# Numerator and transposes side by side in a linear-attention loop, with wo in the numerator's banks

## The chip, the cores and the metric

One Trainium2 chip, one of its cores. The metric is the device time of one execution in microseconds; what is compared is the median over several runs. The engines are named as the profile names them: PE is TensorE, DVE is VectorE, ACT is ScalarE, POOL is GpSimd, SP is SyncE, which issues most of the transfers.

## The reference

Two blocks on a sequence of 2048 tokens with 512 channels. The change touches the first one alone.

```
h = x + A(layernorm(x));   h2 = h + B(layernorm(h))

A: q, k, v = x @ wqkv, 32 heads of 16
   phi(p) = [softmax(p @ w_phi), softmax(-(p @ w_phi))]      per head, 32 features
   num = phi_q (phi_k^T v);   den = phi_q . sum_s(phi_k) + 1e-6
   A = (num / den) @ wo
B: u = gelu(layernorm(h)^T @ w1 + b1)   over tokens, F = 1792;   y = (u @ w2 + b2)^T
```

## The kernel before

The tokens are cut into 16 tiles of 128 (NT = 16). The weights wk and wq are folded with w_phi beforehand. Nearly every product is made as three matmuls of rounded halves (mm3: high x high, high x low, low x high), 128x512 each, so that a projection of one tile is 4 x 3 = 12 matmuls. In the profile these stand at L62, L63 and L64 whatever the product, and are told apart by the tile they write.

**First part (to about 142 us).** For each tile the projections of k (pk_ps), of v (pv) and of some q (pu), the features of k and the products kvp of k and v (L207). Six tiles of q are made here and four more at its end. Of a tile's q logits VectorE takes the maximum and minimum of each head's 16 features (mx, mn), subtracts the maximum (eq), GpSimd makes the negative side (negate, L159 and L160), ScalarE the exponentials (q_exp, L171), and VectorE their sums (q_sum, L216, two reduces), into one PSUM bank that holds eight tiles' sums in turn.

**The loop (142 to about 262 us)** has 19 turns, "it" from 0, in an order written by hand: each engine does its instructions in the order of the code. In one turn these steps stand in the code for different tiles:

- s_tr(it): 16 transposes of the features on TensorE, by halves of 64 rows, into the PSUM tile tn (L528), and two copies of them to pht on ScalarE (L530).
- s_num(it-1): the numerator, 16 small matmuls of 64x32 (32 passes in the profile), also into the PSUM tile tn (L546); ScalarE makes the high half oh (L550), VectorE the low half ol (s_ol, L555).
- s_wo(it-2): 12 matmuls with wo into po (a PSUM bank of its own), and s_h(it-2): VectorE adds the residual and the row's sum (L571), and SP stores it.
- s_moments, s_rstd and s_hn of tile it-3: the second layernorm, on ScalarE, GpSimd and ScalarE again (L577 to L587), and the halves hs of the result (L57 and L58).
- s_den(it+2): the denominator's inverse w, six operations on VectorE in a row (L451 to L457) after GpSimd's ez (s_ez, L442); s_pq multiplies it into the features on GpSimd (L460).
- one more projection of q while there are any (six tiles), and from it = 4 on fill: matmuls of block B's first product, 6 for each tile and pair of columns (pu<-hs). Their weights come by stream: a load on SP, the high half whi on ScalarE (L607) and the low half wlo on VectorE (flush, L599).

VectorE's operations are mixed by turns(): one of the list of ol, logits and sums, one of the denominator, and so on. The PSUM pool ps_t has one buffer of two banks for tn, so transposes and numerator take turns in it and the copies out lie between them.

**After the loop** come the rest of block B's first product and its second product (py), whose code is not changed.

Of the kernel before, what the change touches and what calls it, by code (L numbers as in the profile page):

```python
# [26 lines left out]
SUMS = 8  # L27
# [6 lines left out]
def block_kernel(ctx: ExitStack, tc: tile.TileContext, x, xT, wT, phic, wo, w1, b1, w2, b2,  # L34
# [34 lines left out]
    ps_s = aq.enter_context(tc.tile_pool(name="ps_s", bufs=1, space=PSUM, side="right"))  # L69
    sums = ps_s.tile([P, SUMS, NPR, 2, 2], F32, name="smq")  # L70
# [4 lines left out]
    kvS = wqp.tile([P, 4, 64], F32, name="kvS")  # L75
    wqp.tile([P, 504], F32, name="pad")
# [15 lines left out]
    ps_kv = a1.enter_context(tc.tile_pool(name="ps_kv", bufs=1, space=PSUM))  # L92
    kvp = ps_kv.tile([P, 4, 64], F32, name="kvp")
# [117 lines left out]
    def q_sum(t):  # L211

        assert t < SUMS or t - SUMS in W, "a tile's sums would go where others are still wanted"
        SQ[t] = sums[:, t % SUMS]
        e = signs(EQ[t])
        return [lambda c=c: nc.vector.reduce_sum(SQ[t][:, :, 1 - c], e[:, :, c], axis=AX.X) for c in range(2)]  # L216
# [227 lines left out]
    def s_den(t):  # L444


        tz = az.tile([P, NPR, 2, 2], F32, name="tz")
        den = az.tile([P, NPR, 2], F32, name="den")
        W[t] = az.tile([P, NPR, 2, 2], F32, name="w", bufs=3)
        other = SQ[t]  # L450
        return [lambda: nc.vector.reduce_sum(tz.rearrange("p g c h -> p (g c h)"), heads(EZ[t]), axis=AX.X),  # L451
                lambda: nc.vector.scalar_tensor_tensor(tz[:, :, 0], other[:, :, 1], 1e-6, tz[:, :, 0],
                                                       op0=ALU.mult, op1=ALU.add),
                lambda: nc.vector.tensor_mul(tz, other, tz),
                lambda: nc.vector.reduce_sum(den, tz.rearrange("p g c h -> p g h c"), axis=AX.X),
                lambda: nc.vector.reciprocal(den, den),
                lambda: nc.vector.tensor_mul(W[t], other, den.unsqueeze(2).to_broadcast([P, NPR, 2, 2]))]  # L457
# [3 lines left out]

    def lead(it, mm):

        if 0 <= it + 3 < NT:
            s_ez(it + 3)
        negate()
        for _ in range(mm):
            q_mm()
        q_exp(0)
# [24 lines left out]
    run(s_den(0))  # L494
# [7 lines left out]
    run(s_den(1))  # L502
# [15 lines left out]
    ps_o = a2.enter_context(tc.tile_pool(name="ps_o", bufs=1, space=PSUM, reuse_waits="tile"))  # L518
    HN, HT, PHT, OS, PO, VE = {}, {}, {}, {}, {}, {}

    def s_tr(t):

        PHT[t] = ak.tile([P, NG, P], F32, name="pht")
        ptr = ps_t.tile([P, 2, 4, P], F32, name="tn").rearrange("p r c (a s) -> p r (c a) s", a=2)
        for g in range(NG):
            for r in range(2):
                half = slice(r * 64, r * 64 + 64)
                nc.tensor.transpose(ptr[:, r, g, :], EQ[t][half, g, :], ident[half, half])  # L528
# [3 lines left out]
    def s_kv():  # L532

        pt = ps_o.tile([P, 2, P], F32, name="po")
# [4 lines left out]
    def s_num(t):  # L539

        pn = ps_t.tile([P, 2, 4, P], F32, name="tn")[:, :, 0:2]
        for b in range(2):
            for c in range(4):
                for r in range(2):
                    rows, cols = slice(64 * r, 64 * r + 64), slice(32 * c, 32 * c + 32)
# [11 lines left out]
    def s_wo(t):  # L557
        oh, ol, _ = OS.pop(t)
        PO[t] = po = ps_o.tile([P, D], F32, name="po")
# [34 lines left out]
    LATER = []  # L594

    def flush():
        while LATER:
            wl_, raw, wh_ = LATER.pop(0)
            LO.append(nc.vector.tensor_sub(wl_, raw, wh_).ins)  # L599

    def stream(src, k0, n, c0, w):
# [5 lines left out]
        nc.scalar.activation(wh_, raw, AF.Copy)  # L607
        LATER.append((wl_, raw, wh_))
# [23 lines left out]

    for it in range(NT + 3):
        if 0 <= it < NT:
            s_x(it)
        if 0 <= it - 1 < NT:
            s_num(it - 1)
        if 0 <= it - 3 < NT:
            s_moments(it - 3)
        if 0 <= it - 2 < NT:  # L640
            s_wo(it - 2)
        if it == 1:
            run(q_logits(0))
            q_mm()
        if 0 <= it < NT:
# [3 lines left out]
        if 0 <= it + 1 < NT:  # L649
# [223 lines left out]
```

## Time and profile before

| what | value |
|---|---|
| median of 3 runs | 530.51 us (530.28 to 531.23) |
| the profiled execution | 530.51 us, its span 528.70 us |
| TensorE busy | 521.9 us, 99% of the span, 4000 matmul passes |
| VectorE, ScalarE, GpSimd busy | 72%, 52%, 44% |
| granted TensorE clock | 0.999 |
| median from issue to landing | wraw 2.9 us, h 3.6 us, out<-h 2.0 us |

A row of a timeline gives the start in us from the span's start, the duration, the engine, the line, the operation, what it writes and reads, and in brackets how long the engine had been idle and what ended that. Matmuls are pipelined: their durations overlap, and the distance between starts is what counts. A busy share is an average over parts with different limits.

### The profile page before, as it was taken

What the parts mean: (1) busy time and instruction counts of PE and PEld (TensorE: products, weight loads), DVE (VectorE), ACT (ScalarE), POOL (GpSimd) and SP (SyncE); (2) the same over time, 40 slices, a digit from 0 to 9 for tenths busy, and PEclk for the clock granted to TensorE, in tenths of its full rate; (3) what the DMA queues carried; (4) which work ended last, traced back from release to release, by engine and by line L of the source; (5) the groups of instructions that cost most, each with busy time, mean ns of one, the idle gap of its engine ahead of it and who ended that gap; (6) DMA issues with size and microseconds to landing.
All of it is one profiled execution on the core that took longest, in us unless ns stands there. A gap on an engine that the chain in (4) does not pass through costs nothing.

```text
span 528.7 us, 10143 instructions
## 1 busy us (share of the span) xinstructions
PE 521.9 (99%) x4000; PEld 445.5 (84%) x4000; DVE 379.6 (72%) x680; ACT 272.7 (52%) x460; POOL 231.3 (44%) x190
## 2 busy tenths in 40 slices
PE   8999999999999999999999999999999999999996
PEld 7888888887877777777788888888899999999996
DVE  6993999876899888863426424825668878887784
ACT  6998834525247777676657323526444243343340
POOL 2589699876999988994335000000001101101110
PEclk9999999999999999999999999999999999999999
DMA  8644310012303223333255333533014555535631
GB/s 308 192 129 119 87 35 21 1 49 93 102 1 100 72 97 114 121 121 120 81 183 156 104 98 98 165 115 81 20 41 113 141 146 145 131 125 121 160 75 47
DMA packets 45488, 55.86 MB, mean 106 GB/s; under 512 B 3968, under 2 KB 33024, under 8 KB 45440
## 3 DMA queue, kind: packets, MB, share of 16 engines
q1 hardware_dynamic: 43136, 51.38, 31.0%
q0 software_dynamic: 2016, 3.67, 5.1%
q8 instruction: 31, 0.51, 0.4%
q10 hardware_dynamic: 288, 0.17, 0.1%
q14 instruction: 17, 0.14, 0.1%
HBM read 46.81 MB, written 8.39 MB: 104 GB/s over the span
## 4 chain that ended last, share of the span: by engine, by line
PE 96%; DVE 2%; ACT 0%; issue 0%; DVEq 0%
PE py L767 26%; PE pu L62 13%; PE pu L63 12%; PE pu L64 12%; PE po L62 3%; PE pv L63 3%; PE pv L64 3%; PE pv L62 3%; PE po L63 3%; PE po L64 3%; PE pk_ps L62 2%; PE pk_ps L64 2%; PE pk_ps L63 2%; PE tn L546 2%; PE tn L528 2%; PE kvp L207 2%
## 5 line engine op out<-in xcount | busy, mean ns | idle before, releaser
L805 POOL DMA_DIRECT2D out<-ot x14 | 12.5, 998 | 211.7 <-DVE ot L803 211.7
L767 PE MATMUL py<-uf,whi 128*128 128x256 f32 x560 | 96.2, 283 | 0.0
L62 PE MATMUL pu<-hs,whi 128*128 128x512 f32 x224 | 88.0, 396 | 0.0
L57 ACT ACTIVATE whi<-wraw 128x1792 fp32r<-128x1792 f32 x28 | 47.7, 1704 | 77.9 <-PE py L767 67.2
L63 PE MATMUL pu<-hs,whi 128*128 128x512 f32 x224 | 87.5, 391 | 0.0
L64 PE MATMUL pu<-hs,wlo 128*128 128x512 f32 x224 | 87.0, 390 | 0.2 <-DVE wlo L599 0.2
L767 PEld LDWEIGHTS py<-uf,whi 128*128 128x128 f32 x560 | 83.3, 192 | 0.0
L599 DVE TENSOR_TENSOR wlo<-wraw,whi 128x512 fp32r<-128x512 f32 x56 | 45.5, 823 | 48.7 <-ACT whi L607 48.3
L767 PE MATMUL py<-uf,wlo 128*128 128x256 f32 x280 | 69.9, 283 | 0.0
L58 DVE TENSOR_TENSOR wlo<-wraw,whi 128x1792 fp32r<-128x1792 f32 x28 | 56.6, 2022 | 17.2 <-ACT whi L57 17.1
L607 ACT ACTIVATE whi<-wraw 128x512 fp32r<-128x512 f32 x56 | 34.4, 626 | 45.5 <-PE pu L63 41.4
L64 PEld LDWEIGHTS pu<-hs,wlo 128*128 128x128 f32 x224 | 42.1, 188 | 9.6 <-DVE wlo L599 0.6
L62 PEld LDWEIGHTS pu<-hs,whi 128*128 128x128 f32 x224 | 42.0, 188 | 9.4
L767 PEld LDWEIGHTS py<-uf,wlo 128*128 128x128 f32 x280 | 49.7, 192 | 0.0
L63 PEld LDWEIGHTS pu<-hs,whi 128*128 128x128 f32 x224 | 42.1, 188 | 8.3
L442 POOL TENSOR_TENSOR ez<-eq,zB 128x1024 f32<-128x1024 f32 x16 | 39.3, 2458 | 3.9 <-ACT zB L489 3.9
L767 PE MATMUL py<-un,whi 128*128 128x256 f32 x224 | 38.4, 283 | 0.0
L195 POOL TENSOR_TENSOR pk<-pk,sk 128x1024 f32<-128x1024 f32 x16 | 31.0, 1942 | 9.8 <-DVE sk L194 9.0
L767 PEld LDWEIGHTS py<-un,whi 128*128 128x128 f32 x224 | 33.2, 192 | 0.1
L530 ACT ACTIVATE pht<-tn 128x512 f32<-128x512 f32 x32 | 17.4, 596 | 29.5 <-PE tn L528 29.5
L460 POOL TENSOR_TENSOR eq<-eq,w 128x1024 f32<-128x1024 f32 x16 | 31.0, 1940 | 3.0 <-DVE w L457 3.0
L199 POOL TENSOR_TENSOR zacc<-zacc,pk 128x1024 f32<-128x1024 f32 x13 | 31.3, 2407 | 0.6
(165 smaller groups left out, 1176.0 us busy)
## 6 DMA issues: line engine op xcount, KB each, us to landing
wraw<-in_w SPq DMA_DIRECT2D x112, 256.0 KB, 2.9
xraw<-in_xT SPq DMA_DIRECT2D x16, 256.0 KB, 3.0
xh<-in_x SPq DMA_DIRECT2D x16, 256.0 KB, 2.7
h<-in_x SPq DMA_DIRECT2D x16, 256.0 KB, 3.6
out<-h SPq DMA_DIRECT2D x16, 256.0 KB, 2.0
out<-ot POOLq DMA_DIRECT2D x14, 256.0 KB, 4.8
wraw<-in_wT SPq DMA_DIRECT2D x12, 256.0 KB, 5.0
wo<-in_wo SPq DMA_DIRECT2D x4, 256.0 KB, 3.6
```

What stands on the lines that cost most here:

```text
L57: nc.scalar.activation(hi, src, AF.Copy)
L58: lo_engine.tensor_sub(lo, src, hi)
L62: nc.tensor.matmul(o, ah, bh, start=first, stop=False)
L63: nc.tensor.matmul(o, ah, bl, start=False, stop=False)
L64: nc.tensor.matmul(o, al, bh, start=False, stop=last)
L195: nc.gpsimd.tensor_mul(heads(PK[t]), heads(PK[t]), sk.unsqueeze(2).to_broadcast([P, 2 * H, DH]))
L199: nc.gpsimd.tensor_add(zacc, zacc, PK[t])
L442: nc.gpsimd.tensor_mul(EZ[t], EQ[t], zB)
L460: nc.gpsimd.tensor_mul(heads(EQ[t]), heads(EQ[t]), W[t].rearrange("p g c h -> p (g c h)").unsqueeze(2).to_broadcast([P, 2 * H, DH]))
L599: LO.append(nc.vector.tensor_sub(wl_, raw, wh_).ins)
L607: nc.scalar.activation(wh_, raw, AF.Copy)
L767: nc.tensor.matmul(o, a[x], b[:, y], start=start and i == 0, stop=stop and i == 2, skip_group_check=True)
```

## The change

- The PSUM pools of the loop are now ps_t, two banks for the transposes (tr), and ps_n, two banks for the numerator (pn); s_wo writes po into the numerator's banks. The bank of the sums is given up: the sums of all 16 tiles go to SBUF.
- In a turn s_num(it-1) and s_tr(it) stand directly behind each other; then six matmuls of other work (half a q projection, or a fill), then s_wo(it-1), the tile of the numerator just made, then the other six or twelve, then s_h(it-1). The moments and what follows are those of it-2. Q_TURNS spreads six q projections over eight turns, in halves of six matmuls.
- s_den keeps its temporary values in PSUM, in the transposes' banks once they are copied out (before the loop in a bank of the pool ps_d), and its six operations now follow each other, between the two reduces of the sums.
- A streamed weight's high half is made in his(), on ScalarE after s_hn, and its low half in flush at the turn's end, after s_h.

The lines' numbers move with it: the denominator stands at L454 to L462, s_pq at L465, whi at L600 and wlo at L606.

```diff
...
 V_NOT = (0, 1, 11)
-SUMS = 8
+Q_TURNS = ((0, 1), (0, 1), (0, 1), (0, 1), (0,), (1,), (0,), (1,))
 LAG = 4
...
     ps_q = ctx.enter_context(tc.tile_pool(name="ps_q", bufs=2, space=PSUM, side="right"))
-    ps_s = aq.enter_context(tc.tile_pool(name="ps_s", bufs=1, space=PSUM, side="right"))
-    sums = ps_s.tile([P, SUMS, NPR, 2, 2], F32, name="smq")
     wqp = aq.enter_context(tc.tile_pool(name="wqp", bufs=1, side="right"))
...
     kvS = wqp.tile([P, 4, 64], F32, name="kvS")
+    sums = wqp.tile([P, NT, NPR, 2, 2], F32, name="smq")
     wqp.tile([P, 504], F32, name="pad")
...
     ps_kv = a1.enter_context(tc.tile_pool(name="ps_kv", bufs=1, space=PSUM))
+    ps_d = a1.enter_context(tc.tile_pool(name="ps_d", bufs=1, space=PSUM))
     kvp = ps_kv.tile([P, 4, 64], F32, name="kvp")
...
-        assert t < SUMS or t - SUMS in W, "a tile's sums would go where others are still wanted"
-        SQ[t] = sums[:, t % SUMS]
+        SQ[t] = sums[:, t]
         e = signs(EQ[t])
...
-    def s_den(t):
-        tz = az.tile([P, NPR, 2, 2], F32, name="tz")
-        den = az.tile([P, NPR, 2], F32, name="den")
+    def s_den(t, pool, name):
         W[t] = az.tile([P, NPR, 2, 2], F32, name="w", bufs=3)
         other = SQ[t]
-        return [lambda: nc.vector.reduce_sum(tz.rearrange("p g c h -> p (g c h)"), heads(EZ[t]), axis=AX.X),
-                lambda: nc.vector.scalar_tensor_tensor(tz[:, :, 0], other[:, :, 1], 1e-6, tz[:, :, 0],
+        at = []
+        def first():
+            bank = pool.tile([P, 8, P], F32, name=name)[:, 0] if name == "tr" else pool.tile([P, P], F32, name=name)
+            at.extend((bank[:, 0:64].rearrange("p (g c h) -> p g c h", c=2, h=2),
+                       bank[:, 64:96].rearrange("p (g h) -> p g h", h=2)))
+            nc.vector.reduce_sum(at[0].rearrange("p g c h -> p (g c h)"), heads(EZ[t]), axis=AX.X)
+        return [first,
+                lambda: nc.vector.scalar_tensor_tensor(at[0][:, :, 0], other[:, :, 1], 1e-6, at[0][:, :, 0],
                                                        op0=ALU.mult, op1=ALU.add),
-                lambda: nc.vector.tensor_mul(tz, other, tz),
-                lambda: nc.vector.reduce_sum(den, tz.rearrange("p g c h -> p g h c"), axis=AX.X),
-                lambda: nc.vector.reciprocal(den, den),
-                lambda: nc.vector.tensor_mul(W[t], other, den.unsqueeze(2).to_broadcast([P, NPR, 2, 2]))]
+                lambda: nc.vector.tensor_mul(at[0], other, at[0]),
+                lambda: nc.vector.reduce_sum(at[1], at[0].rearrange("p g c h -> p g h c"), axis=AX.X),
+                lambda: nc.vector.reciprocal(at[1], at[1]),
+                lambda: nc.vector.tensor_mul(W[t], other, at[1].unsqueeze(2).to_broadcast([P, NPR, 2, 2]))]
...
         nc.gpsimd.tensor_mul(heads(EQ[t]), heads(EQ[t]), W[t].rearrange("p g c h -> p (g c h)").unsqueeze(2).to_broadcast([P, 2 * H, DH]))
-    def lead(it, mm):
-        if 0 <= it + 3 < NT:
-            s_ez(it + 3)
-        negate()
-        for _ in range(mm):
-            q_mm()
-        q_exp(0)
...
     v_kv()
-    run(s_den(0))
+    run(s_den(0, ps_d, "dn"))
     run(q_logits(0))
...
     v_kv()
-    run(s_den(1))
+    run(s_den(1, ps_d, "dn"))
     run(q_logits(0))
...
     ps_t = a2.enter_context(tc.tile_pool(name="ps_t", bufs=1, space=PSUM, reuse_waits="tile"))
-    ps_o = a2.enter_context(tc.tile_pool(name="ps_o", bufs=1, space=PSUM, reuse_waits="tile"))
+    ps_n = a2.enter_context(tc.tile_pool(name="ps_n", bufs=1, space=PSUM, reuse_waits="tile"))
     HN, HT, PHT, OS, PO, VE = {}, {}, {}, {}, {}, {}
...
+    HALF = [slice(64 * r, 64 * r + 64) for r in range(2)]
+    def banks(name):
+        return ps_n.tile([P, 2, 4, P], F32, name=name, tag="pn")
     def s_tr(t):
         PHT[t] = ak.tile([P, NG, P], F32, name="pht")
-        ptr = ps_t.tile([P, 2, 4, P], F32, name="tn").rearrange("p r c (a s) -> p r (c a) s", a=2)
+        ptr = ps_t.tile([P, 8, P], F32, name="tr").rearrange("p (r c) (a s) -> p r (c a) s", r=2, a=2)
         for g in range(NG):
-            for r in range(2):
-                half = slice(r * 64, r * 64 + 64)
-                nc.tensor.transpose(ptr[:, r, g, :], EQ[t][half, g, :], ident[half, half])
+            for r, rows in enumerate(HALF):
+                nc.tensor.transpose(ptr[:, r, g, :], EQ[t][rows, g, :], ident[rows, rows])
         for r in range(2):
...
-        pt = ps_o.tile([P, 2, P], F32, name="po")
+        pt = banks("pt")[:, 0, 0:2]
         for b in range(2):
...
-        pn = ps_t.tile([P, 2, 4, P], F32, name="tn")[:, :, 0:2]
+        pn = banks("pn")[:, :, 0:2]
         for b in range(2):
             for c in range(4):
-                for r in range(2):
-                    rows, cols = slice(64 * r, 64 * r + 64), slice(32 * c, 32 * c + 32)
+                for r, rows in enumerate(HALF):
+                    cols = slice(32 * c, 32 * c + 32)
                     nc.tensor.matmul(pn[cols, r, b, :], kvB[rows, b, cols], PHT[t][rows, 4 * b + c, :],
...
         oh, ol, _ = OS.pop(t)
-        PO[t] = po = ps_o.tile([P, D], F32, name="po")
+        PO[t] = po = banks("po")[:, 0].rearrange("p a s -> p (a s)")
         for j in range(4):
...
-    LATER = []
+    COMING, LATER = [], []
+    def his():
+        while COMING:
+            LATER.append(COMING.pop(0))
+            _, raw, wh_ = LATER[-1]
+            nc.scalar.activation(wh_, raw, AF.Copy)
...
     def flush():
+        his()
         while LATER:
...
         nc.sync.dma_start(raw, src[:, k0:k0 + n, c0:c0 + w])
-        nc.scalar.activation(wh_, raw, AF.Copy)
-        LATER.append((wl_, raw, wh_))
+        COMING.append((wl_, raw, wh_))
         return wh_, wl_
...
+    def q_half(i):
+        t = q["mm"]
+        if i == 0:
+            PS[t] = ps_q.tile([P, D], F32, name="pu", tag="pu")
+        for kt in range(2 * i, 2 * i + 2):
+            mm3(PS[t], X[t][:, 0, kt, :], X[t][:, 1, kt, :], wqh[:, kt, :], wql[:, kt, :], kt == 0, kt == KD - 1)
+        q["mm"] += i
+    def turn(it):
+        halves = Q_TURNS[it] if it < len(Q_TURNS) else ()
+        n = [FN[0] <= it - LAG and FN[0] < NT, min(2, max(0, it - LAG + 1 - FN[1])) if q["logits"] == NT else 0]
+        for p in range(2):
+            if it >= LAG - 2 + 2 * p and FL[p] < min(NT, FN[p] + n[p] + 1 + p):
+                fill_load(p)
+        return ([lambda i=i: q_half(i) for i in halves] + [lambda: fill(0, ps_f)] * n[0]
+                + [lambda: fill(1, ps_q)] * n[1])
     for it in range(NT + 3):
-        if 0 <= it < NT:
+        if it < NT:
             s_x(it)
+        shifted = q["logits"] - len(MN)
+        ql = q_logits(0)
+        work = turn(it)
+        if 0 <= it - 2 < NT:
+            s_moments(it - 2)
         if 0 <= it - 1 < NT:
             s_num(it - 1)
-        if 0 <= it - 3 < NT:
-            s_moments(it - 3)
-        if 0 <= it - 2 < NT:
-            s_wo(it - 2)
-        if it == 1:
-            run(q_logits(0))
-            q_mm()
-        if 0 <= it < NT:
+        if it < NT:
             s_tr(it)
...
             s_kv()
-        if 0 <= it + 1 < NT:
+        if it + 1 < NT:
             s_pq(it + 1)
-        if 0 <= it - 3 < NT:
-            s_rstd(it - 3)
-        lead(it, 1)
-        den = s_den(it + 2) if it + 2 < NT else []
-        ql = q_logits(1)
-        ops = turns((s_ol(it - 1) if 0 <= it - 1 < NT else []) + ql + (q_sums(0) if it > 0 else []), den)
-        at = 7 if ql else 3
-        ops[at:at] = [flush]
-        ops[3:3] = [lambda: s_h(it - 2)] if 0 <= it - 2 < NT else []
-        run(ops)
-        if it > 0:
-            negate()
-        if 0 <= it - 3 < NT:
-            s_hn(it - 3)
-        if FN[0] <= it - LAG:
-            fill(0, ps_f)
-        for _ in range(2):
-            if q["logits"] == NT and FN[1] <= it - LAG:
-                fill(1, ps_q)
-        for p in range(2):
-            if it >= LAG - 2 and FL[p] <= FN[p] + 1:
-                fill_load(p)
+        for w in work[:1]:
+            w()
+        if q["exp"] < shifted:
+            q_exp(0)
+        if 0 <= it - 2 < NT:
+            s_rstd(it - 2)
+        if it + 3 < NT:
+            s_ez(it + 3)
+        if 0 <= it - 2 < NT:
+            s_hn(it - 2)
+        negate()
+        his()
+        sm = q_sums(0) if q["sum"] <= it + 3 else []
+        run(ql[:2] + (s_ol(it - 1) if 0 <= it - 1 < NT else []) + ql[2:] + sm[:1])
+        run(s_den(it + 2, ps_t, "tr") if it + 2 < NT else [])
+        run(sm[1:])
+        if 0 <= it - 1 < NT:
+            s_wo(it - 1)
+        for w in work[1:]:
+            w()
+        if 0 <= it - 1 < NT:
+            s_h(it - 1)
+        flush()
     flush()
...
```

## The prediction

> **What bounds the kernel now.** The profiled execution took 530.51 us, a span of 528.70 and 1.81 around it; the median of the three runs is 530.51 too, so the sum below is made against 530.51. First the page: busy times, slices, chain.
>
> ```profile
> PE 521.9 (99%) x4000; PEld 445.5 (84%) x4000; DVE 379.6 (72%) x680; ACT 272.7 (52%) x460; POOL 231.3 (44%) x190
> PE   8999999999999999999999999999999999999996
> DVE  6993999876899888863426424825668878887784
> PE 96%; DVE 2%; ACT 0%; issue 0%; DVEq 0%
> ```
>
> TensorE has no hole after the first 20 us, and 96% of the chain is its own work. Its matmuls are the same after the change, so time can be won only where one follows another too slowly, and lost wherever TensorE begins to wait. The changed loop runs from 142.5 to about 262 us, where VectorE's slices stand at 8 and 9: the second engine is close behind. Next, TensorE's timeline: two plain projections, and one turn of the loop.
>
> ```profile
> 122.08 0.39 PE L62 MATMUL pv<-wvh,xs 128*128 128x512 f32 x1
> ...
> 124.80 0.39 PE L62 MATMUL pu<-wqh,xs 128*128 128x512 f32 x1
> ...
> 199.24 0.39 PE L64 MATMUL pu<-hs,wlo 128*128 128x512 f32 x1
> 199.56 0.67 PE L546 MATMUL tn<-pht,kvB 64*32 64x128 f32 x32
> 200.16 0.50 PE L62 MATMUL po<-woh,oh 128*128 128x512 f32 x1
> 200.50 0.40 PE L63 MATMUL po<-wol,oh 128*128 128x512 f32 x1
> ...
> 202.78 0.39 PE L64 MATMUL po<-woh,ol 128*128 128x512 f32 x1
> 203.10 0.71 PE L528 MATMUL tn<-ident,eq 64*128 64x64 f32 x16
> 203.74 0.50 PE L62 MATMUL pu<-hs,whi 128*128 128x512 f32 x1
> ```
>
> Starts count, not durations (they overlap). Twelve plain matmuls take 124.80-122.08 = 2.72, 0.227 each. The twelve after the numerator take 203.10-200.16 = 2.94: 0.22 more, of which 0.09 is the step into the small tiles (202.78 to 203.10 is 0.32) and 0.13 the way out (0.34 from the first to the second). The twelve after the transposes (196.58 to 199.56) take 2.98: 0.09 in, 0.17 out. A turn is 0.60+2.94+0.64+2.98 = 7.17.
>
> Then VectorE and ScalarE, for what will stand in a row:
>
> ```profile
> 132.56 1.22 DVE L451 TENSOR_REDUCE tz<-ez 128x64 f32<-128x1024 f32 x1 [3.38 <-POOL ez L442]
> ...
> 135.08 0.68 DVE L151 TENSOR_REDUCE mx<-pu 128x32 f32<-128x512 f32 x1
> 157.15 0.68 DVE L571 SCALAR_TENSOR_TENSOR h<-po,h 128x512 f32<-128x512 f32 x1
> 157.76 0.08 DVE L571 DVE_READ_ACCUMULATOR h<-po,h 128x1 f32 x1
> ```
>
> ```profile
> 177.05 0.60 ACT L550 ACTIVATE oh<-tn 128x512 fp32r<-128x512 f32 x1 [0.99 <-PE tn L546]
> 177.54 0.19 ACT L577 ACTIVATE ve<-ve 128x1 f32<-128x1 f32 x1
> 177.77 0.72 ACT L578 ACTIVATE hj<-h,ve 128x512 f32<-128x512 f32 x1
> 178.62 0.29 ACT L579 ACTIVATE ve<-ve,eps 128x1 f32<-128x1 f32 x1
> ```
>
> The denominator's six operations without others between them cost 2.52 (132.56 to 135.08). The residual's sum is ready 0.69 after its start. The three moments cost 1.3 (177.54 to 178.62, and about 0.2). A 512-wide VectorE operation occupies 0.60 (157.15 to the next at 157.76).
>
> **The change, part by part. Merging.** In turns 1 to 15 the numerator runs straight into the transposes: one way out (0.13) and one step in (0.09) go, 15 x 0.22 = 3.3 us. The price of going from one small shape to the other is read at the only such place:
>
> ```profile
> 141.48 1.10 PE L207 MATMUL kvp<-pk,vs 128*32 128x64 f32 x64
> 142.51 0.71 PE L528 MATMUL tn<-ident,eq 64*128 64x64 f32 x16
> ```
>
> 1.03 from start to start, and 1.03 also where a projection follows kvp (118.20 to 119.23): no charge of its own. I take 0 (bounds: 0.09 less, if the drain behind the numerator is spared, to 0.22 more, if all is paid again). The Trainium skill, page "TensorEngine Tiling (Array Packing)", Key Properties, says that changing the tiling mode, not just the tile, drains TensorE, and 64x32 to 64x128 is a change of mode; read as a whole switch paid again it leaves the merge no saving where TensorE leads, rival 3's 533.6. [...]
>
> A turn of 24 matmuls becomes 6.95. Turns 8 to 11, now with 30, become 8.31 and have slack on every engine. TensorE's wait of 0.43 in the before (the twelve from 188.98 take 3.41, not 2.98, behind a late wlo) goes, because the weights' halves are now made a turn ahead. Gains: 3.3+0.43 = 3.75.
>
> **Head.** den(2) now lies in the transposes' banks, so tr(1) waits for it. In turn 0 VectorE does kvS (142.65), max, min, shift (142.99 to 144.78) and 2.52 of denominator: W ends at 147.38, TensorE restarts at 147.43. It would have reached tr(1) at 146.28+0.60 = 146.88. Cost 0.55; nothing hides it.
>
> **The ring.** h(t-1) reads po, which lies in the banks that num(t) writes, so num waits for h, and the whole turn of TensorE is queued behind num. In the order of the built program h stands behind all of that turn's VectorE work, and on ScalarE the moments of the same tile stand ahead of oh. From one h's end to the next: signal 0.05 (0.03 from ScalarE's oh, 161.96, to ol, 161.99; 0.09 from w, 154.45, to pq, 154.54), moments 1.29, oh 0.60, signal 0.04, ol 0.61, shift 0.60, first sum 0.59, denominator 2.52, second sum 0.59, h 0.69: 7.58. Maximum and minimum (1.2) fit into the 1.98 before ol. That is 0.63 over TensorE's 6.95. Turns 3, 4 and 6 have all of it: 1.9. Turn 2 enters with about 0.4 of slack and pays 0.25. Turns 5 and 7 have no logits: 6.98, together 0.1. Sum 2.25. From turn 8 on logits meet 8.31; from 12 on there are neither sums nor logits, and 5.8 is under 6.95.
>
> Moving the sums to SBUF and tz, den to PSUM I cost at nothing: a 512-wide reduce takes 0.68 from PSUM to SBUF (L151) and 0.68 from SBUF to PSUM (L216). For the dependent small steps the trace has only SBUF results; bounds -0.05 to +0.10 for each of five, so -0.25 to +0.5 a turn in some seven turns; I take 0, since the small ones with a PSUM input (0.22, L454) equal those without (0.22, L455).
>
> **The port.** wlo now comes right after h, ahead of the next maximum, while GpSimd is at its busiest (pq 1.90, power and product 0.76, ez 2.35, hs 1.24, negation 1.35: 7.6 a turn in turns 2 to 5).
>
> ```profile
> 189.14 2.08 DVE L599 TENSOR_TENSOR wlo<-wraw,whi 128x512 fp32r<-128x512 f32 x1
> ```
>
> Alone it takes 0.68 (199.46); here it stood behind ez until 190.67. With 0.68+1.2 = 1.9 of the 1.98 filled, nearly any wait shifts ol. It matters in turns 3 and 6, at 0 to 1.4 each; GpSimd should then be in its 1.06 to 1.29 operations, part done, so I take 0.5 in all. The Trainium skill, page "SBUF — State Buffer", section "SBUF: two separate sides", calls the pair of ports an exclusive lock, held for the whole instruction, between GpSimd and a VectorE operation with two SBUF inputs; the row agrees (2.08 against 0.68).
>
> **Tail.** In turn 16 only six matmuls stand between numerator and wo, 0.60+0.11+1.36 = 2.07, while ol is ready 0.78 (160.58 to oh at 161.36) +0.60+0.04+0.69+0.06 = 2.17 after its start: 0.1. In turn 17 ScalarE makes whi of the last pair behind moments(15) and hn(15). From wo's last start: 0.49 to h (0.39 of matmul, 0.10 as from numerator to oh), 0.69, 0.05, moments 1.37, GpSimd's power and product 0.86, hn 0.90, hs 0.54, whi 0.62, 0.06: 5.58. TensorE has 19 x 0.227 = 4.31 of work until it needs it: 1.27. Restarting twice at 0.34 in place of 0.23 adds 0.2. Sum 1.55.
>
> **Queues.** Moments, rstd and hn come a turn earlier relative to their tile, with the same operations; SP's loads and stores move with their turns, out(t) goes a turn earlier ahead of the next loads, and loads land in 2.9 (wraw) and 3.6 us (h) against turns of 7: nothing. Past 262 us TensorE's work and order by kind stay.
>
> **Sum.** -3.75 +0.55 +2.25 +0.5 +1.55 = +1.1: I forecast 531.6, with 530.9 to 532.4 for this case alone.
>
> **Rivals.** (1) Faster: the ring does not bind. If its steps overlap by 0.63 or more (signals, or wlo and small operations cheaper), turns 2 to 7 run at 6.95 and only head and tail stay: 530.5-3.75+0.55+1.55 = 528.85. For it: 2.52 is from SBUF results, and VectorE is busy 72% on average. Against: every step is a true dependence or a queue order, and the slices say 8 and 9. (2) Slower: the small steps in PSUM cost 0.06 more each, 0.3 in seven turns, 2.1: 533.7; or turns 3 and 6 pay the port in full, +2.3: 533.9. (3) The shape switch is paid in full: turns 1 and 8 to 15, where TensorE leads, lose 9 x 0.22 = 2.0: 533.6. Against it: the kvp row.
>
> **Numbers.** Measurement tells about 0.2%, 1.06 us, from no change. The forecast has 0.65, and straddles +1.06: 0.34 within, 0.31 slower. Rival 1 has 0.14, rival 2 0.16, rival 3 0.05. Faster 0.14, same 0.34, slower 0.52. The range 529.2 to 533.7 reaches into rivals 1 and 2.
>
> **What would show it.** Right: num followed by tr 0.60 later with no gap; turns 1 and 8 to 15 at 6.95 and 8.31; turns 3, 4, 6 near 7.6 with TensorE waiting for h at num; a wait of about 0.55 at tr(1), and of 1.3 for whi before pu at the loop's end. Wrong: turns 3, 4 and 6 at 6.95 (rival 1), a denominator over 2.7 from reduce to sum (rival 2), num to tr over 0.75 (rival 3), or any difference past the loop.

## The result, and the profile after

The changed kernel takes 531.68 us (median of 19 runs, 531.09 to 532.37) against 530.54 for the kernel before on the same chip (19 runs, 530.28 to 531.39): a ratio of 1.0017, 95% interval 1.0010 to 1.0024. The profiled execution took 532.08, a span of 530.3.

From the page of the changed kernel: busy times, VectorE's slices, the chain.

```profile
PE 520.0 (98%) x4000; PEld 447.1 (84%) x4000; DVE 381.6 (72%) x680; ACT 272.6 (51%) x460; POOL 231.5 (44%) x190
...
DVE  6893999976889988685235424835758877978774
...
PE 87%; DVE 6%; ACT 4%; issue 2%; POOL 1%; DVEq 0%; ACTq 0%; POOLq 0%
```

TensorE has 1.9 us less of busy time (521.9 before), and VectorE's slices in the loop, the 11th to 16th, stand at 8 and 9 as before (the 17th and 18th are 6 and 8, where they were 8 and 6). But only 87% of the chain is now TensorE's own work, against 96%: it has begun to wait. The list of TensorE's waits says for whom (us in total, times, longest):

```profile
PE pn L546 <- DVE h L571: 2.1, 4, 0.7
PE pu L62 <- ACT whi L600: 1.1, 1, 1.1
...
PE tr L528 <- DVE w L462: 0.6, 1, 0.6
```

Those are the ring, the tail and the head of the prediction. The same places in TensorE's timeline:

```profile
146.91 0.67 PE L546 MATMUL pn<-pht,kvB 64*32 64x128 f32 x32
148.18 0.71 PE L528 MATMUL tr<-ident,eq 64*128 64x64 f32 x16 [0.60 <-DVE w L462]
...
168.42 0.39 PE L64 MATMUL pu<-wqh,xs 128*128 128x512 f32 x1
169.47 0.67 PE L546 MATMUL pn<-pht,kvB 64*32 64x128 f32 x32 [0.66 <-DVE h L571]
170.07 0.71 PE L528 MATMUL tr<-ident,eq 64*128 64x64 f32 x16
...
238.93 0.67 PE L546 MATMUL pn<-pht,kvB 64*32 64x128 f32 x32
239.53 0.71 PE L528 MATMUL tr<-ident,eq 64*128 64x64 f32 x16
240.17 0.50 PE L62 MATMUL pu<-hs,whi 128*128 128x512 f32 x1
...
268.58 0.39 PE L64 MATMUL pu<-hs,wlo 128*128 128x512 f32 x1
270.08 0.50 PE L62 MATMUL pu<-hs,whi 128*128 128x512 f32 x1 [1.11 <-ACT whi L600]
```

Numerator to transposes is 0.60 where nothing is waited for (238.93 to 239.53): the change of shape has no price of its own. Behind 168.42 the numerator would start 0.32 later if it waited for nothing; it starts 1.05 later, since h is late. At 268.58 the distance is 1.50 instead of 0.23.

VectorE's and ScalarE's rows of turn 4 are the ring, link by link:

```profile
168.64 0.68 DVE L571 SCALAR_TENSOR_TENSOR h<-po,h 128x512 f32<-128x512 f32 x1
...
171.25 0.69 DVE L555 TENSOR_TENSOR ol<-pn,oh 128x512 fp32r<-128x512 f32 x1 [0.73 <-ACT oh L550]
...
173.06 1.22 DVE L454 TENSOR_REDUCE tr<-ez 128x64 f32<-128x1024 f32 x1
...
175.60 0.68 DVE L215 TENSOR_REDUCE smq<-eq 128x32 f32<-128x512 f32 x1
176.20 0.68 DVE L571 SCALAR_TENSOR_TENSOR h<-po,h 128x512 f32<-128x512 f32 x1
```

```profile
169.36 0.20 ACT L577 ACTIVATE ve<-ve 128x1 f32<-128x1 f32 x1 [2.53 <-DVE h L571]
...
170.64 0.58 ACT L550 ACTIVATE oh<-pn 128x512 fp32r<-128x512 f32 x1
```

From h to h it is 176.20-168.64 = 7.56, where 7.58 was summed: h to the moments 0.72, moments 1.28 (169.36 to 170.64), oh to ol 0.61, ol to the denominator 1.81 (ol, shift, first sum), the denominator 2.54, the second sum 0.60.

Turn by turn (from the start of one numerator to the next, us), with two of the kernels that follow:

| turn | 1 | 2 | 3 | 4 | 5 | 6 | 7 | 8 to 11 | 12 to 15 |
|---|---|---|---|---|---|---|---|---|---|
| before | 7.14 | 7.17 | 7.17 | 8.53 | 8.53 | 7.59 | 7.17 | 7.17 | 7.17 |
| changed | 7.57 | 7.22 | 7.77 | 7.56 | 6.97 | 7.93 | 6.97 | 8.28 | 6.91 |
| apart (below) | 7.55 | 8.11 | 8.12 | 8.11 | 8.11 | 8.11 | 8.11 | 8.59 | 7.69 |
| last version | 7.31 | 6.90 | 6.93 | 6.90 | 6.93 | 6.90 | 7.02 | 8.28 | 6.92 |

(The turns hold different numbers of matmuls, so the first row compares with the others only in sum.) The first transpose of the loop starts at 142.51 before and 143.12 after; in the profiled executions of the changed kernel and its twelve variants that start lies anywhere from 142.34 to 143.24, though the code ahead of it is the same in twelve of the thirteen. So the loop is measured from there to the first py: 240.23 before, 241.46 after, +1.23. The spans of the two profiled executions differ by 1.6: 0.61 is that start, 1.23 the loop, and behind the first py the changed kernel's is 0.2 shorter.

### The profile page after: what moved, and what is told of

It reads as the page before. It is cut to its first block, busy times and chain, and to the rows that moved or that the text cites. A ratio compares the mean times of both kernels' runs of the same rounds, so it can differ in the third digit from the quotient of the medians.

```text
span 530.3 us, 10156 instructions
## 1 busy us (share of the span) xinstructions
PE 520.0 (98%) x4000; PEld 447.1 (84%) x4000; DVE 381.6 (72%) x680; ACT 272.6 (51%) x460; POOL 231.5 (44%) x190
## 4 chain that ended last, share of the span: by engine, by line
PE 87%; DVE 6%; ACT 4%; issue 2%; POOL 1%; DVEq 0%; ACTq 0%; POOLq 0%
PE py L790 26%; PE pu L62 11%; PE pu L63 11%; PE pu L64 11%; PE pv L63 3%; PE pv L64 3%; PE pv L62 3%; PE pk_ps L62 2%; PE pk_ps L64 2%; PE pk_ps L63 2%; PE po L64 2%; PE po L62 2%; PE po L63 2%; PE kvp L207 2%; PE tr L528 1%
## 5 line engine op out<-in xcount | busy, mean ns | idle before, releaser
L606 DVE TENSOR_TENSOR wlo<-wraw,whi 128x512 fp32r<-128x512 f32 x56 | 44.2, 796 | 49.7 <-ACT whi L600 49.5
L600 ACT ACTIVATE whi<-wraw 128x512 fp32r<-128x512 f32 x56 | 34.6, 625 | 47.9 <-PE pu L63 43.7
L465 POOL TENSOR_TENSOR eq<-eq,w 128x1024 f32<-128x1024 f32 x16 | 32.8, 2052 | 1.7 <-DVE w L462 1.4
L790 PE MATMUL py<-un,wlo 128*128 128x256 f32 x112 | 27.6, 283 | 0.0
```

The source lines that it names most:

```text
L465: nc.gpsimd.tensor_mul(heads(EQ[t]), heads(EQ[t]), W[t].rearrange("p g c h -> p (g c h)").unsqueeze(2).to_broadcast([P, 2 * H, DH]))
L790: nc.tensor.matmul(o, a[x], b[:, y], start=start and i == 0, stop=stop and i == 2, skip_group_check=True)
```

## Experiments

Each is an edit on the changed kernel unless said otherwise. "To it" is the difference of the medians, each taken against the kernel before in its own set of runs (530.54 to 531.00); "in the trace" is the stretch from first transpose to first py, against 241.46.

| kernel | median us | ratio to before, 95% | to it | in the trace |
|---|---|---|---|---|
| changed | 531.68 | 1.0010 to 1.0024 | | |
| high half first in the tail | 529.97 | 0.9978 to 0.9996 | -1.8 | -1.63 |
| second sum behind h | 529.94 | 0.9976 to 0.9994 | -1.8 | -1.63 |
| numerator and transposes apart | 540.12 | 1.0164 to 1.0192 | +8.3 | +8.50 |
| turn 0: shift behind den | 531.79 | 1.0008 to 1.0025 | 0.0 | -0.17 |
| apart, other bank in turns 0 to 3 | 538.97 | 1.0140 to 1.0177 | +7.2 | +7.21 |
| other turns for the loads | 532.88 | 1.0028 to 1.0054 | +1.1 | +0.72 |
| turn 0: den in an idle bank | 531.21 | 1.0004 to 1.0022 | -0.6 | -0.32 |
| four edits together | 528.15 | 0.9943 to 0.9968 | -3.6 | -3.75 |
| ... and rstd's product on ScalarE | 528.35 | 0.9946 to 0.9971 | -3.8 | -3.29 |
| ... and ol first in turn 1 | 530.08 | 0.9975 to 0.9993 | -2.0 | -2.07 |
| den's temporaries in SBUF | 543.11 | 1.0208 to 1.0259 | +11.0 | +12.35 |
| last version | 527.30 | 0.9921 to 0.9949 | -4.8 | -4.63 |

**The tail.** In turns 17 and 18 the high halves that are still to be made go ahead of the moments on ScalarE.

```diff
         work = turn(it)
+        if it > NT:
+            his()
         if 0 <= it - 2 < NT:
             s_moments(it - 2)
```

> The changed kernel, but past the last turn with a tile of its own (it 17 and 18) the high half of the streamed weight is made ahead of the moments on ScalarE instead of behind hn. Nothing else moves. Theory of the tail: TensorE waits 1.27 us there because whi stands behind moments, rstd and hn of tile 15; ScalarE is idle before moments(15) and the weight has long landed, so whi (0.62) fits in that idle time and the wait goes: 1.3 us less than the changed kernel, about 530.4, and the gap of 1.50 between two matmul starts at the loop's end becomes 0.23 to 0.35. Rival: the transfer of the weight is late, or TensorE only meets the next wait (h of tile 15, hn, the low half): 531.7, the gap stays above 1.0 or appears again a few matmuls later.

Measured -1.8 (trace -1.63). ScalarE's rows:

```profile
262.05 1.14 ACT L600 ACTIVATE whi<-wraw 128x512 fp32r<-128x512 f32 x2
264.85 0.20 ACT L577 ACTIVATE ve<-ve 128x1 f32<-128x1 f32 x1 [1.66 <-DVE h L571]
```

The second of those two whi is the one that stood at 269.41 in the changed kernel, behind hs; now it lies in time that ScalarE waits for h anyway. No wait for whi is left in the list, and no distance over 0.24 between matmul starts follows. The gain is over 1.27 because the restart behind the gap goes as well: in the changed kernel the matmuls after 270.08 stand further apart than 0.227 for some 2.5 us, by 0.11 at first, 0.23 in all; together that is 1.50 of the trace's 1.63. The transfer was never late.

**The ring.** The second reduce of the sums goes behind h.

```diff
         run(s_den(it + 2, ps_t, "tr") if it + 2 < NT else [])
-        run(sm[1:])
         if 0 <= it - 1 < NT:
             s_wo(it - 1)
...
             s_h(it - 1)
+        run(sm[1:])
         flush()
```

> The changed kernel, but the second reduce of the logits' sums goes behind h in VectorE's order, so that only shift, first sum and denominator stand between ol and h. Same work, same engines. Theory of the ring: TensorE waits at the numerator because h(t-1) is late, and everything ahead of h on VectorE counts in full: the ring shortens by 0.59. In turn 4 that brings 7.56 down to TensorE's 6.95; in turns 3 and 6, where wlo follows h too, the reduce now stands between h and the next ol (wlo 0.68 + sum 0.59 + max and min 1.2 = 2.5 against 1.98 of room), so ol comes about 0.5 later and little is left of the gain. In all 0.6 to 1.2 us less: 530.5 to 531.1. Rival, VectorE's throughput: its work per turn is what binds, and where a reduce stands changes nothing: 531.7, turn 4 stays at 7.5.

Measured -1.8, more than expected. TensorE's rows of the end of turn 4:

```profile
174.97 0.39 PE L64 MATMUL pu<-hs,wlo 128*128 128x512 f32 x1
175.34 0.67 PE L546 MATMUL pn<-pht,kvB 64*32 64x128 f32 x32
```

The wait for h is gone (0.37 instead of 1.05), and in the whole list: turns 2 to 7 take 6.90, 7.50, 6.97, 6.90, 7.30 and 7.21. The same work stands on the same engine, so in turns 2 and 4 VectorE's throughput doesn't set the time; its order does. (In turns 3 and 6 of the changed kernel VectorE has no pause from one h to the next, so there its work counts too.) Turns 3 and 6 don't reach 6.95, as expected, since wlo, the sum, maximum and minimum don't fit into the room ahead of ol; but they gain 0.27 and 0.63 where "little" was expected, turn 2 gains 0.32 that the expectation left out, and turn 7 loses 0.24 (ol waits 1.71 for ScalarE's oh there; "Together" has the same wait).

**The merge.** From turn 1 on the transposes go behind the first six matmuls of other work.

```diff
-        if it < NT:
+        if it == 0:
             s_tr(it)
...
         for w in work[:1]:
             w()
+        if 0 < it < NT:
+            s_tr(it)
```

> The changed kernel, but in turns 1 to 15 the transposes come behind the first six matmuls of other work instead of right behind the numerator: each group of small tiles now stands alone among the 128x512 matmuls. Banks, halves and VectorE's order are as in the changed kernel. Theory: a second step into and out of the small tiles costs 0.22 a turn, but it shows only where TensorE leads (turns 1 and 8 to 15, 9 x 0.22 = 2.0); in turns 2 to 7 TensorE waits for h anyway and the cost is swallowed by that wait. 533.7, turns 8 to 11 at 8.53 and 12 to 15 at 7.15, turns 3 and 4 unchanged. Rival a: the step costs wherever it is, 15 x 0.22 = 3.3: 535.0. Rival b: the saving of the merge comes from the banks and not from the order; apart costs nothing: 531.7.

Measured +8.3: neither the theory nor a rival. Where TensorE leads (turns 8, 9, 11 and 15) a turn is longer by 0.24 to 0.25, as expected, 8.53 and 7.17. But turns 2 to 7 and 12 take 8.11: something new binds. (Turn 13, at 7.53, ends in a wait for h; turn 14, at 7.96, holds one for wlo, and turn 10, at 8.79, one for ol.) TensorE, ScalarE and VectorE in one such turn:

```profile
170.35 0.67 PE L546 MATMUL pn<-pht,kvB 64*32 64x128 f32 x32 [0.91 <-DVE h L571]
...
172.54 0.71 PE L528 MATMUL tr<-ident,eq 64*128 64x64 f32 x16
...
178.46 0.67 PE L546 MATMUL pn<-pht,kvB 64*32 64x128 f32 x32 [0.88 <-DVE h L571]
```

```profile
173.29 1.09 ACT L530 ACTIVATE pht<-tr 128x512 f32<-128x512 f32 x2 [1.20 <-PE tr L528]
```

```profile
174.47 1.23 DVE L454 TENSOR_REDUCE tr<-ez 128x64 f32<-128x1024 f32 x1 [0.46 <-POOL ve L583]
...
177.63 0.68 DVE L571 SCALAR_TENSOR_TENSOR h<-po,h 128x512 f32<-128x512 f32 x1
```

The denominator starts 0.09 after the transposes are copied out (173.29+1.09 = 174.38), because its values lie in their banks. The name in the bracket, GpSimd's ve, had ended at 174.05. So there is a ring through TensorE: numerator, six matmuls and transposes 2.19, copies 0.75 and 1.09, denominator 0.09 and 2.56, sum 0.60, h 0.68, numerator 0.15: 8.11.

**The bank.** To show it: apart as above, but the denominator's values of turns 0 to 3 in a bank of ps_f, idle until turn 4 (and in s_den a tile of that name and shape for it).

```diff
-        run(s_den(it + 2, ps_t, "tr") if it + 2 < NT else [])
+        run(s_den(it + 2, *((ps_f, "pu") if it <= 3 else (ps_t, "tr"))) if it + 2 < NT else [])
```

> The kernel with numerator and transposes apart (540.1, turns 2 to 7 at 8.11), but in turns 0 to 3 the denominator's values lie in a bank that stands idle until turn 4, in place of the transposes' banks; from turn 4 on they lie there as before. Theory: apart is slow because the denominator may begin only when the transposes are copied out, and the chain num, six matmuls, transposes, copies, denominator, sum, h, num goes round in 8.11. With the bank elsewhere turns 2 and 3 fall back to the ring of the changed kernel, 7.2 to 7.8, and turns 4 to 7 stay at 8.11; tr(1) no longer waits either: 537.5 to 539.0. Rival: apart costs by the exponentials behind the later copies, or by the copies that the numerator waits for; then the bank changes nothing and turns 2 and 3 stay at 8.11: 540.1 or 0.3 less.

Measured 538.97, 1.15 less than apart. VectorE's rows of turns 3 and 4:

```profile
165.56 1.21 DVE L455 TENSOR_REDUCE pu<-ez 128x64 f32<-128x1024 f32 x1
...
173.65 1.23 DVE L455 TENSOR_REDUCE tr<-ez 128x64 f32<-128x1024 f32 x1 [0.45 <-POOL eq L466]
```

In the other bank the denominator begins without a pause, in the transposes' banks it waits 0.45 again. Turn 2 falls to 7.22, turns 4 to 7 stay at 8.10 to 8.11. Turn 3 falls to 8.00 only: there wlo takes 1.35 behind GpSimd, and ol is late for that (the step from transposes to wo is 0.13 longer). The mechanism is shown; the size expected for turn 3 was wrong.

**The head, twice.** First, in turn 0 the denominator goes ahead of the shift; then the shift stays where it was, and the denominator's values lie in the idle bank.

```diff
-        run(ql[:2] + (s_ol(it - 1) if 0 <= it - 1 < NT else []) + ql[2:] + sm[:1])
+        run(ql[:2] + (s_ol(it - 1) if 0 <= it - 1 < NT else []) + (ql[2:] if it else []) + sm[:1])
         run(s_den(it + 2, ps_t, "tr") if it + 2 < NT else [])
+        run([] if it else ql[2:])
```

> The changed kernel, but in turn 0 VectorE makes the denominator of tile 2 ahead of the shift of the logits instead of behind it. Theory of the head: tr(1) waits 0.60 for w of tile 2, because the denominator's values lie in the transposes' banks, and the wait is set by what VectorE does before it; with 0.60 of shift moved behind, the wait goes: 0.6 us less, 531.1, and tr(1) follows its numerator by 0.60 with no gap. Rival: the shift is then late for the negative side and the exponentials of that tile (GpSimd and ScalarE), whose sums are wanted from turn 1 on, and the 0.6 come back as a wait in turns 1 or 2: 531.7.

Measured 0.0. The wait of tr(1) halves, from 0.60 to 0.26, and no more, for the same reason as with the two apart: the copies out of the bank; then ol, behind the shift, is late for wo by 0.17. VectorE and ScalarE:

```profile
143.46 0.68 DVE L152 TENSOR_REDUCE mn<-pu 128x32 f32<-128x512 f32 x1
144.31 1.23 DVE L454 TENSOR_REDUCE tr<-ez 128x64 f32<-128x1024 f32 x1 [0.17 <-issue]
```

```profile
143.13 1.09 ACT L530 ACTIVATE pht<-tr 128x512 f32<-128x512 f32 x2 [2.88 <-PE tr L528]
```

The denominator could have begun at about 144.06; it begins 0.09 after the copies' end at 144.22.

> The changed kernel, but in turn 0 alone the values of the denominator of tile 2 lie in a bank that stands idle until turn 4. Theory of the head: tr(1) waits for w of tile 2 because of the bank alone; the wait of 0.67 goes, and turn 1 takes 6.9. How much of it is kept depends on the ring: h(0) of turn 1 stands behind VectorE's work, which does not become shorter, so turn 2 should give some back, from 7.22 to 7.5: 0.3 to 0.67 less than the changed kernel, 531.0 to 531.4. Rival: VectorE sets the time from turn 0 on, and all of it is given back in turn 2: 531.7.

This is the edit of "The bank", with `it <= 0`. Measured -0.6 (trace -0.32). tr(1) no longer waits and turn 1 takes 7.28 instead of 7.57, not 6.9: ol, behind the maximum and minimum, is now what wo waits for (0.24). Turn 2 stays at 7.22; what is given back is given back in turn 1.

**The port.** The streamed weights in other turns.

```diff
-            if it >= LAG - 2 + 2 * p and FL[p] < min(NT, FN[p] + n[p] + 1 + p):
+            if (it, p) in ((1, 0), (4, 0), (6, 1)) or it > 6 and FL[p] < min(NT, FN[p] + n[p] + 1 + p):
```

> The changed kernel, but the first three streamed weights are loaded in turns 1, 4 and 6 instead of 2, 4 and 5 (the one for the second pair of columns last), so that the low halves wlo are made at the start of turns 2, 5 and 7 instead of 3, 5 and 6. In turns 5 and 7 there are no maximum and minimum ahead of ol, and turn 1 leaves VectorE idle for 0.65. Theory of the port: wlo between h and the next maximum, stretched by GpSimd to 1.12 and 1.28, sets ol back in turns 3 and 6; without it these turns fall from 7.77 and 7.93 to the ring's 7.56: 0.4 to 0.6 less in all, 531.1 to 531.3. Rival: ol has room there and the two turns are long for the ring alone, or wlo delays turn 2 as much: 531.7.

Measured +1.1: the wrong sign. Turns 3 and 6 do fall, from 7.77 and 7.93 to 7.56 and 7.56, but turn 2 grows from 7.22 to 8.60. VectorE and GpSimd there:

```profile
153.44 2.34 DVE L606 TENSOR_TENSOR wlo<-wraw,whi 128x512 fp32r<-128x512 f32 x1
...
156.90 0.68 DVE L555 TENSOR_TENSOR ol<-pn,oh 128x512 fp32r<-128x512 f32 x1
```

```profile
153.29 1.94 POOL L465 TENSOR_TENSOR eq<-eq,w 128x1024 f32<-128x1024 f32 x1
```

GpSimd's 1.94 had begun 0.15 before wlo, and wlo ended 0.55 behind its end: it takes 1.66 more than the undisturbed 0.68. In the version with four edits the same wlo begins at 153.35, 0.17 before that GpSimd operation, and takes 0.76. A third of a microsecond decides between the whole price and none.

**Den in SBUF.** The denominator's temporaries where they were before the change; the sums stay in SBUF.

```diff
-        at = []
+        at = [az.tile([P, NPR, 2, 2], F32, name="tz"), az.tile([P, NPR, 2], F32, name="den")]
         def first():
-            bank = ...
-            at.extend(...)
```

> The changed kernel, but the denominator's temporary values lie in SBUF, as they did before the change, while the sums stay in SBUF too. Three of its small steps then have two SBUF inputs, as wlo has. tr(1) no longer waits for it. Theory of the port: each such step waits, like wlo, for the GpSimd operation under way, and GpSimd is busy nearly all the time in turns 2 to 6; the spacing from the denominator's reduce to the next operation grows from 2.55 to 4 to 7, all of it in the ring: 1.5 to 4 a turn in five turns or more, 537 to 552. Then the move of the denominator to PSUM is what lets the sums leave it. Rival: steps of 0.2 slip in between GpSimd's operations, 2.55 to 2.7, and the head's wait goes: 531.0 to 531.5.

Measured +11.0. Three small steps of one turn:

```profile
169.56 0.63 DVE L454 SCALAR_TENSOR_TENSOR tz<-smq,tz 128x32 f32<-128x32 f32 x1
170.22 1.25 DVE L456 TENSOR_TENSOR tz<-smq,tz 128x64 f32<-128x64 f32 x1
...
172.15 0.66 DVE L459 TENSOR_TENSOR w<-smq,den 128x64 f32<-128x64 f32 x1
```

```profile
167.72 2.41 POOL L441 TENSOR_TENSOR ez<-eq,zB 128x1024 f32<-128x1024 f32 x1
170.10 1.28 POOL L58 TENSOR_TENSOR hs<-hn,hs 128x512 fp32r<-128x512 f32 x1
```

These steps take 0.20, 0.23 and 0.22 with one input in PSUM; their means over the loop are 0.49, 0.78 and 0.55. The first two end 0.06 and 0.09 behind GpSimd's ez (170.13) and hs (171.38). From the reduce to the next operation it is 4.42 here (168.31 to 172.73) instead of 2.55. The Trainium skill, page "SBUF — State Buffer", section "SBUF: two separate sides", has this as an exclusive lock between GpSimd and a VectorE operation with two SBUF inputs; the rows agree, down to operations of 0.2.

The 11.0 are the median of two runs that lie 2.4 apart (541.91 and 544.31, the profiled one), and they are not all in the ring. The list of waits and the granted clock of that execution:

```profile
PE pn L543 <- DVE h L568: 7.1, 7, 2.4
PE pt L533 <- DVE kvS L501: 1.8, 1, 1.8
...
PEclk9999999999899899999999999999999999999999
```

The waits for h are 5.0 longer in all than in the changed kernel, and 1.8 is new at the loop's start: kvS stands on VectorE behind the denominator of tile 1, of which one step takes 2.36 (140.00). The wait of 0.6 at tr(1) is gone. These come to 6.2 of the trace's 12.35. About as much again goes with the clock: at or just behind the three longest waits (1.83, 2.40 and 1.97) the granted clock stands at 0.50, for 3.4, 6.8 and 3.4 us (from 146.4, 173.7 and 201.0), and matmuls start 0.43 apart instead of 0.23. TensorE works for 13.1 us of them at half the clock, which makes about 6.5 (an estimate). In the loops of the other kernels of this case it stays at 1.00. So turns 3 to 7 take 7.6 to 9.8, and the longest, turn 4, is long for the clock: no wait stands at its end. What made the clock fall, no run here tests.

**Together.** Tail, second sum, loads and idle bank in turn 0, and nothing else.

> All four edits on the changed kernel: the high half ahead of the moments at the loop's end, the second sum behind h, the loads in turns 1, 4 and 6, the denominator of turn 0 in an idle bank. Theory: each removes a wait of TensorE of its own, so the gains add up: 1.27 at the tail, 0.67 at the head, and in turns 2 to 7 the ring (7.0) and the late ol go, 7.22, 7.77, 7.56, 6.97, 7.93 and 6.97 to 6.9 to 7.0 each: 2.5 to 3.0. In all 4.4 to 4.9 less: 526.8 to 527.3, TensorE without a wait of over 0.1 in the loop. Rival: VectorE's throughput in turns 1 to 4 (some 6.9 of work in 6.9) keeps one or two of the waits: 528.0 to 528.5.

Measured 528.15, the gain to the changed kernel 3.6 of the 4.4 to 4.9. Turns 2 to 6 take 6.90 to 6.93; turn 7 takes 7.95. GpSimd and ScalarE ahead of it:

```profile
186.83 0.55 POOL L583 TENSOR_TENSOR r<-ve,mhalf 128x1 f32<-128x1 f32 x1
```

```profile
187.69 0.82 ACT L588 ACTIVATE hn<-h,ve,r 128x512 f32<-128x512 f32 x1 [1.52 <-POOL ve L584]
...
189.07 0.61 ACT L601 ACTIVATE whi<-wraw 128x512 fp32r<-128x512 f32 x1
...
190.86 0.58 ACT L551 ACTIVATE oh<-pn 128x512 fp32r<-128x512 f32 x1
```

GpSimd has no pause from 147.92 on, and its turns of 7.6 to 8.1 fall behind TensorE's 6.9 by 0.7 to 1.2 each. Here its rstd is so late that ScalarE's hn, and in its queue whi, moments and oh, come late for ol. The rival gave the number, but named the wrong engine.

```diff
-        nc.gpsimd.tensor_mul(VE[t][:, 1:2], VE[t][:, 1:2], r2[:, t:t + 1])
+        nc.scalar.activation(VE[t][:, 1:2], VE[t][:, 1:2], AF.Identity, scale=r2[:, t:t + 1])
```

> The kernel with all four edits (528.15), but the product of mean and rstd, GpSimd's second small operation of rstd (0.19, and 0.33 from its start to the next one's with the pause ahead of it), is made on ScalarE in front of hn. In the kernel with four edits GpSimd runs without a pause from 147.9 to beyond 192, its turns take 7.6 to 8.1 against TensorE's 6.9, and in turn 7 (7.95) rstd comes so late that ScalarE gets to the moments and to oh 1.2 late. Theory: GpSimd is the third bound; five turns at 0.33 less bring rstd of turn 7 forward by 1.6, the 1.05 of turn 7 goes, 527.1 to 527.4. Rival: turn 7 is late for VectorE or for the weight's load, or the product on ScalarE only moves the wait: 528.1.

Measured 528.35, no gain. Counted from the loop's first transpose (142.34 here, 142.94 with four edits), rstd of turn 7 at 185.71 comes 0.5 earlier and not 1.6: a turn saves 0.25, not 0.33, and GpSimd now waits 0.45 for hs once. Turn 7 falls to 7.51; but wlo, behind whi, now meets GpSimd's next operation and takes 1.76, and another of 1.45 makes turn 8 8.95.

```diff
-        run(ql[:2] + (s_ol(it - 1) if 0 <= it - 1 < NT else []) + ql[2:] + sm[:1])
+        ol = s_ol(it - 1) if 0 <= it - 1 < NT else []
+        run((ol + ql[:2] if it == 1 else ql[:2] + ol) + ql[2:] + sm[:1])
```

> As the kernel with the product on ScalarE, but in turn 1 alone ol goes ahead of the maximum and minimum on VectorE. Theory: turn 1 takes 7.27 because ol stands behind two operations that are not urgent there, and wo waits 0.24 for it; ahead of them ol is ready by about 0.8 earlier and the wait goes: 0.2 to 0.3 less than that kernel, 526.8 to 527.2. Rival: ol would then wait for oh, VectorE stands idle for it, h(0) comes later by as much and turn 2 pays: no gain or 0.2 more.

Measured 530.08, 1.7 more. wo no longer waits in turn 1, but h(0) is late instead (turn 1 still 7.24), and the wlo behind it now begins at 154.04, 0.20 after GpSimd's 1.93, and takes 2.28: turn 2 takes 8.34. The last one is without this edit:

```diff
+        if it > 3:
+            his()
         if 0 <= it - 2 < NT:
             s_rstd(it - 2)
```

> As the kernel with the product on ScalarE (528.35), but from turn 4 on the high half of the streamed weight is made on ScalarE ahead of rstd's product and hn instead of behind hs, where ScalarE waits 1.25 for GpSimd anyway. In that kernel turn 7 takes 7.51: wlo begins 0.49 late behind whi, meets GpSimd's next operation and takes 1.76, and ol and wo wait. Theory: with whi ready early, wlo follows the second sum at once, waits only for the rest of GpSimd's product ez and is done a microsecond before ol is due; turn 7 falls to 6.9 to 7.0, and the total by about 0.5, to 527.8. Turn 8 (8.95, its wlo of 1.45 begins right behind the sum already) is left as it is, or changes with where GpSimd stands then. Rival: wlo meets another GpSimd operation, in turn 7 or 8, and takes as long again: 528.0 to 528.7.

Measured 527.30: faster than the kernel before by 3.7 (ratio 0.9935, 0.9921 to 0.9949) and than the changed one by 4.8. TensorE's list of waits has nothing of the loop left; only turn 1, at 7.31, still loses some 0.4 where wo follows a late ol. VectorE and GpSimd in turn 7:

```profile
188.39 1.09 DVE L607 TENSOR_TENSOR wlo<-wraw,whi 128x512 fp32r<-128x512 f32 x1
190.20 0.69 DVE L556 TENSOR_TENSOR ol<-pn,oh 128x512 fp32r<-128x512 f32 x1 [0.72 <-ACT oh L551]
```

```profile
188.89 1.74 POOL L58 TENSOR_TENSOR hs<-hn,hs 128x512 fp32r<-128x512 f32 x1
```

wlo follows at once and is done 0.7 before ol can start. This time GpSimd pays: hs takes 1.74, not 1.28. Turn 8 fell to 8.28 with it, by luck of where GpSimd stood (wlo 0.75), not by the edit's reason.

How full GpSimd is can be read from the busy times by stretch (us, then PE, PEld, DVE, ACT and POOL busy), here the changed kernel from 149 to 185:

```profile
149.00:185.00 36.00, 34.51 (x356) 26.66 (x357) 32.95 (x68) 25.41 (x50) 34.79 (x31) 1.00 0.24 77
```

GpSimd is busy for 34.79 of 36 us, more than TensorE's 34.51, while the page of the profile has GpSimd at 44%. (An operation held up by VectorE, 2.39 us instead of 1.94, counts as busy in full.)

## Why the prediction came out right, point by point

The forecast was +1.1 and 531.6; the loop has +1.23, the median is 531.68. By its steps:

- **Merging**, 0.22 a turn and no price for the change of shape: shown. Numerator to transposes 0.60; turns 12 to 15 at 6.91 (6.95 forecast), 8 to 11 at 8.28 (8.31); taken apart again, 0.24 to 0.25 a turn where TensorE leads. Rival 3 falls. The Trainium skill, page "TensorEngine Tiling (Array Packing)", Key Properties, says that a change of tiling mode drains TensorE. The trace has extra time at the steps into and out of the 128x512 matmuls (0.09 and 0.13), and none between these two small shapes (0.60 from numerator to transposes, as from numerator to a 128x512 matmul before); the row of kvp, 1.03 whatever follows, could show only that the two steps cost alike.
- **Head**: 0.67 where 0.55 was summed. The cause was named, the bank. Of the 0.12 over, 0.10 is the signal: from the end of w (147.81+0.22 = 148.03) to the transposes at 148.18 it is 0.15, where 0.05 was taken. That the denominator must also wait for the copies out of that bank was missed. It cost nothing here (the copies end at 144.97, the shift ahead of the denominator at 145.40), but it explains 8.11 in turns 2 to 7 when the transposes come later: with the denominator in those banks, the transposes have to stand right behind the numerator.
- **Ring**: 7.56 in turn 4 against 7.58, turn 2 at 7.22 (0.27 over 6.95, 0.25 forecast), turns 5 and 7 at 6.97. The second sum moved behind h shows for turns 2 and 4 that it is this chain and not VectorE's throughput. Rival 1 falls.
- **Port**: turns 3 and 6 lie 0.21 and 0.37 above turn 4's 7.56; without their wlo they take 7.56. Sum 0.58, forecast 0.5. GpSimd was in its 1.06 us operation in turn 3 and in its 1.29 us one in turn 6, as the forecast had it. That 0.5 out of 0 to 2.8 came so near is partly luck: in other variants a wlo at the start of turn 2 took 0.76 and 2.34, begun at nearly the same moment.
- **Small steps in PSUM at nothing**: 2.54 to 2.55 against 2.52. With the port at 0.58 and not 2.8, both halves of rival 2 fall. What the prediction didn't price is the way not taken: with sums and temporaries both in SBUF it was +11.0, about half of it waits and half the lower clock.
- **Tail**: the gap of 1.27 to the hundredth, and 0.1 at wo of turn 16 (0.317 where 0.227 is usual). With the slow restart the experiment gave 1.6 to 1.8, forecast 1.55 in all.
- **Left out**: GpSimd. Its 7.6 a turn was in the text, for the port alone. Against a turn of 6.95 it is a bound of its own, hidden as long as the ring of 7.56 slowed the turns; it showed as soon as the ring was gone.

So the gain from merging was real, and it went into four waits of TensorE: h, the halves of a weight twice (on ScalarE and on VectorE), and a bank. That the loop and the median come within 0.13 and 0.08 of the forecast is partly luck: the starts of the loop alone differ by up to 0.9 between executions.

## What to carry to other kernels

When the leading engine is full, a change that saves time on it is paid by the engines behind it: sum their chains from one use of a shared buffer to the next, in the order of each queue, and compare with the new, shorter turn. Move whatever the chain doesn't need behind its last link: one reduce moved by one place was worth as much as the whole tail. And a buffer that is borrowed brings its owner's dependencies along, so ask what else must be over before it is free.

## What the runs showed that was not expected

- Where GpSimd and a VectorE operation with two SBUF inputs meet, a third of a microsecond decides over 1.5 us: wlo takes 0.76 when it begins 0.17 before GpSimd's product with w, 2.34 and 2.28 when it begins 0.15 and 0.20 behind it. In the first case GpSimd takes 2.39 instead of 1.94. Such a price is a draw of lots, and an edit elsewhere, even a good one, draws again: the other turns for the loads alone lost 1.1, ol first lost 1.7.
- After the gap of 1.50 TensorE is slower for some 2.5 us: 0.34, 0.28 and several of 0.24 to 0.25 between starts instead of 0.227.
- In the kernel with the denominator's temporaries in SBUF the granted clock stood at 0.50 for 3.4 to 6.8 us at each of TensorE's three longest waits in the loop (1.83 to 2.40); behind the wait of 1.11 at the changed kernel's loop end it stayed at 1.00.
- The start of the loop differs by up to 0.9 us between profiled executions whose code up to it is the same.
